# Routed attention and a mixture layer in one kernel: spare score banks in h's PSUM region, split cluster products, centroids on another queue, a new hand-written order

## The chip, the cores and the metric

The kernel runs on one core of one Trainium2 chip. The metric is device time in microseconds of one execution; smaller is better. The engines are TensorE (PE; its weight loads are shown as PEld), VectorE (DVE), ScalarE (ACT), GpSimd (POOL) and SyncE (SP), which here only issues transfers. SBUF holds 128 partitions; PSUM, where TensorE writes, has eight banks of 512 float32 per partition.

## The reference

Attention with 4 batches, 8 heads, 768 tokens and head size 64. Every query and key is assigned to the nearest of 16 centroids of its head, and a query sees only the keys of its own cluster. The result, 3072 tokens of 512, goes through a layer with a softmax-weighted activation and a layer norm.

```
q_n, k_n, c_n = each divided by its own norm
q_assign = argmax(q_n . c_n);  k_assign = argmax(k_n . c_n)
scores = q k^T / 8, where q_assign == k_assign, else -1e9
x = softmax(scores) v            # (3072, 512)
h = x w_in                       # (3072, 1024)
solu = h * softmax(h)
ln = (solu - mean) / sqrt(var + 1e-6) * g_ln
out = ln w_out                   # (3072, 512)
```

## The kernel before

**Tiling.** Heads are worked in pairs: 4 batches of 4 pairs, written b.p. A pair's queries and keys lie in one of six `qk` buffers with rows for the 64 features and, beneath them, one-hot rows of the cluster. The product of two such columns holds the score and a large constant where the clusters agree, and the exponential with a bias of the same size then makes all other keys vanish. So the mask costs no instruction of its own, but scores of a pair can start only when its one-hot rows are placed.

**Scores.** They are made in 294 banks of up to 512 columns, in the fixed order of the list `BANKS` (line 254 on): 24 banks for pair 0.0, then 54 for the pairs 0.1 to 0.3 (first 18 banks for the token thirds 0 and 1 of all three, six of a pair and third at a time, so that pair 0.1 has banks 24 to 35, pair 0.2 36 to 47, pair 0.3 48 to 59; then third 2 of each), then the other batches. TensorE writes a bank (S, line 582), ScalarE takes its exponential (E, line 588), and TensorE multiplies it with v (V, line 605); DVE divides by the sums (N, lines 617 and 630). The score banks come from a pool of three (`ps_s`, line 213), so bank i waits until the exponential of bank i - 3 has read its buffer (`ring_s`, line 1001).

**The layer.** It is done in 24 blocks f of 128 tokens. x is turned by a DMA transpose (tx; the last one by TensorE, ptx); h is four pieces of two matmuls (h, line 691) into `hreg`, a PSUM region of three banks, of which even f use banks 0 and 1 and odd f banks 1 and 2. DVE takes the negative maximum (hm, line 697), ScalarE the exponential (ex, line 703), DVE the product u (line 710) and its statistics (bn, ag), GpSimd the scale (at, al), a DMA transposes u (tu; the last two blocks by TensorE, ptu), TensorE makes y in four parts of two matmuls (y, line 757), ScalarE or DVE scales it (sc), and SP sends it out (ou).

**Preparation of a pair.** Loads (ld, lv on SP); a transpose, by TensorE into `hreg` with a copy out for batch 0 (tp, line 384; xa, line 394), by DVE for the others (xt, line 408); four casts into `qk` (ca, lines 432 to 436); a product with the centroids (cl, lines 446 and 451) in PSUM; its turn, maximum, comparison and turn on DVE (tb, mx, oh, ot, lines 460 to 484); four copies that place the one-hot rows (pl, lines 496 to 503: TensorE's batch 0, line 496; else 503, or line 501 by DMA); a blank (bl, line 512); v's casts (cv, line 521). Pair 0.0 is done in two halves of its tokens. For pairs 0.1 to 0.3 the cluster product has 8 matmuls in a row, in float32, at one go.

**Weights.** w_in is loaded (li) and cast on GpSimd (wi, line 540). w_out is loaded (lo), DVE sums its rows weighted by g_ln (su, line 560), TensorE makes the mean of the sum with one matmul of 512 columns into bank 2 of `hreg` (me, line 565), and DVE subtracts it from each of eight blocks (ce0 to ce7, line 568).

**What sets the order.** The class `Weave` (line 23). Every operation is added once with its engine, what it needs and how it is emitted. `ORDER` gives, per engine, the sequence of kinds by hand: `S3 V2 h` means three score banks, two V, one h, each the next of its kind. `AWAY` moves single operations to another engine than their usual one. Each engine executes its queue strictly in that order; an instruction that waits holds everything behind it.

**Start.** SP issues the centroids' load (line 791), then loads of pair 0.0 (line 367) alternate between ScalarE's queue and SP's. DVE normalises the centroids (cn, lines 833 to 846, with one power on GpSimd, line 836); TensorE turns them (cp, line 855).

Of the kernel before, what the change touches and what calls it, by code (L numbers as in the profile page):

```python
# [22 lines left out]
class Weave:  # L23
# [6 lines left out]
        ld4 lv si ld3 lo lg ld3 lv ld lo ld3 lo lv ld4 lv lo li ld8 li3 tx ld4 tx ld2 lv3 tu ld7 tx  # L30
        tu ld8 tu ld3 ou ld lv3 tu ou ld ou ld9 tu ld9 ou tx tu ld tx ld5 lv ld7 tu lv tx ou tu ld7
        tu ou2 ld4 ou ld4 lv ld3 tu2 ld2 pl ou pl2 ld pl tx lv ld2 tu lv ou tx ou lv tu tx pl tu pl2
        ou pl tu2 ou tx tu ou tx3 ou tu2 tx ou tu ou2 tu2 ou6
    """
    ORDER["POOL"] = """
        ca3 cv2 pl bl ca2 pl2 ca2 pl2 ca2 pl z sg ca2 pl2 ca bl pl2 cv z cv ca pl ca2 cv4 pl2 bl pl
        ca3 z ca z2 wi4 ca2 pl4 ca cv3 pl2 at bl al pl2 bl ca cv at ca4 al ca at pl3 ca cv2 pl at al
        cv2 ca2 cv al cv at cv pl4 ca2 cv ca2 pl4 bl at al ca6 al pl3 ca at ca pl bl ca cv al pl ca
        cv pl3 at ca at bl ca5 al cv pl2 at bl pl2 cv al2 ca2 bl cv ca4 at2 al pl cv al pl2 ca pl ca
        pl bl po pl at ca pl ca cv2 pl bl ca2 at2 al2 at3 al2 at al at2 al2 at al2 at al2 at al  # L40
    """
    ORDER["PE"] = """
        wm tp2 cp tp cl tp fl4 cl fl tp2 S3 tp2 S cq S2 tp2 S3 cl V2 S V S2 tp2 gt S V3 S2 tp2 S3 cl
        S2 V2 S V S2 tp S2 tp S V S V S V S3 cl S2 V2 S2 V2 S3 V2 S2 V S V S2 cl S2 V2 S2 V2 S3 V2
        S2 V2 S3 V2 S2 V2 S2 me S2 V2 S2 V2 S2 cl S3 V4 S2 h S h S2 h2 S2 V2 S2 V2 S h2 V2 S2 h S V2
        S2 h2 S3 h V3 S2 y3 S y S2 V3 S2 h2 S3 V4 cl S h2 S2 y S V2 S2 y2 S2 y V S2 V h V S3 V h2 S
        V y V y S3 y V3 S2 V y S V S h S2 h2 S V S2 cl S3 V3 h y2 S V S2 y2 S2 V2 S cl V S3 V4 S h S
        V S2 h S h S2 cl S V2 S2 V2 y2 S2 V2 S V2 S2 y S y S2 V3 S V S2 h2 S h2 S2 h2 S V S V3 y2 S
        y S y h2 S3 V cl V h S2 cl S2 V3 h S3 V3 S h2 S2 y4 S2 V h V3 S3 V h V S2 h S h S V S h S y3
        S3 V4 h V S2 h S y S h S h V2 S cl V2 S3 cl V2 S3 y2 S2 y S V2 h S y V2 S3 V2 cl S2 h2 S3 V  # L50
        y4 S V3 S2 y S y S2 V3 S2 V S y2 S3 V3 S V S h2 S h S2 V h S V2 S h S2 V h S y3 V S3 V y h2
        S2 V2 S V S cl V2 S2 h V h S2 h S h V S2 h S y2 V3 S V2 S2 h S h S2 h V S2 V3 y h V S3 h y V
        S2 h2 V S2 h S V y2 h V2 S3 y2 S2 V h2 S2 V y2 S V2 S2 h y h S2 h2 S2 V3 y S2 V S h2 V3 S V
        h2 S3 y4 h2 S3 V h2 S V3 y2 h y2 V S3 h2 V h y4 h V2 h y4 h2 ptx y4 h2 y3 h2 y ptu2 y7 ptu2
        y5
    """
    ORDER["DVE"] = """
        cn cb tb mx oh ot pl3 tb mx oh ot xa2 cf ca2 bl tb mx oh gk ot N pl su xa su tb mx oh xa ot
        su xa N xt su pl tb mx N oh bl ot xt N su tb su pl N su2 N mx oh ot N xt2 ce2 N ce2 tb N ce3
        hm ce N u mx oh ot N hm xt bn2 ag u xt N bn hm bn xt ag tb u mx N bn oh ot xt2 hm bl N bn u  # L60
        ag xt bn2 ag sc hm N tb mx oh ot u bn2 N xt tb mx bl xt oh N hm ot tb N u mx ag N xt oh bn
        ot N bn xt hm xt ag u xt bn2 ag hm tb N u mx tb oh bn N ot hm xt bn u sc xt N ag mx hm oh
        bn2 u xt2 N hm ag ot tb xt tb N mx u mx xt oh bn ot bn tb N ag bn hm bn sc mx N cv xt oh2 N
# [12 lines left out]
        ca0.0.0.1.1 sc23.0 xa0.0.0.1 xa0.0.1.0 xa0.1.0.0 xa0.1.0.1 xa0.2.0.0 xa0.2.0.1 xa0.2.1.0  # L76
        xa0.2.1.1 xa0.3.0.0
    """.split(), "ACT"))
    AWAY.update(dict.fromkeys("""
        bl0.0.1 bl0.2 bl1.2 bl1.3 bl3.3 ca0.0.1.1.1 ca0.1.0.0 cv3.0.0 cv3.1.0 cv3.3.0 cv3.3.1  # L80
        pl0.0.0.1.1 pl0.1.1.0 pl0.2.0.1 pl0.3.0.0 sc10 sc17 sc19 sc2 sc6 sc9 tu22.0
    """.split(), "DVE"))
    AWAY.update(dict.fromkeys("""
        ca0.0.1.1.0 pl0.0.1.0.0 pl0.0.1.1.0 pl1.0.0.0 pl1.0.0.1 pl1.0.1.0 pl1.0.1.1 pl1.1.0.0
        pl1.1.0.1 pl1.1.1.0 pl1.1.1.1 pl1.2.0.0 pl1.2.0.1 pl1.2.1.0 pl1.2.1.1 pl1.3.0.0 pl1.3.0.1
        pl1.3.1.0 pl1.3.1.1 pl2.0.0.0 pl2.0.0.1 pl2.0.1.0 pl2.0.1.1 pl2.1.0.0 pl2.1.0.1 pl2.1.1.0
        pl2.1.1.1 pl2.2.0.0 pl2.2.0.1 pl2.2.1.0 pl2.2.1.1 pl2.3.0.0 pl2.3.0.1 pl2.3.1.0 pl2.3.1.1
# [1153 lines left out]
```

## Time and profile before

| | us |
|---|---|
| timed runs: median (lowest to highest) | 228.2 (227.93 to 229.53) |
| the profiled execution, its own time | 229.23 |
| its span in the profile | 227.2 |
| PE busy | 216.9 |
| DVE busy | 201.0 |
| ACT busy | 195.0 |
| POOL busy | 132.3 |
| exponentials of the scores (L588), 294 | 152.0 |
| matmuls of the scores (L582), 636 | 93.5 |

The span runs from the first to the last instruction; some 2 us lie outside it. Matmul records overlap one another, so a sum of their durations is more than what they take of the engine. In the view by stretch each engine has its busy time in that stretch, with the count of instructions. In the view of waits a line says which instruction waited for which, the total in us, how often, and the longest. In the chain a line is a start, a length and what the chain passed through. In a list of instructions the columns are start, length, engine, line, operation, output<-input, count, and in brackets the idle time before it with what ended it. In the groups they are busy time and mean ns, then the idle time ahead.

### The profile page before, as it was taken

To read this page: it belongs to the slowest core of one execution; us is meant where nothing else is said; L and a number is where in the kernel's file an instruction comes from. 1 tells how busy PE (TensorE), PEld (TensorE's weight loads), DVE (VectorE), ACT (ScalarE), POOL (GpSimd) and SP (SyncE) were. 2 spreads that over 40 slices of the span, in tenths; PEclk is the share of its full clock that TensorE was granted. 3 is DMA by queue.
4 is the path that set the end of the run, shared out by engine and by line. 5 is a ranking of instruction groups with operands and counts; after the bars stand their busy time and mean duration, and the time that the engine had idled before them with its cause. 6 is when DMAs were issued, how large, how long until landed. Compare 5 with 4: busy or idle time off the path is not lost.

```text
span 227.2 us, 6588 instructions
## 1 busy us (share of the span) xinstructions
PE 216.9 (95%) x2394; PEld 147.8 (65%) x2424; DVE 201.0 (88%) x353; ACT 195.0 (86%) x378; POOL 132.3 (58%) x256
## 2 busy tenths in 40 slices
PE   6999988999999999999999999999999999999993
PEld 2566655666777767686567766687677677675452
DVE  2699999999999899898999989899899969798991
ACT  3599989999999999999888999899999999974352
POOL 4587799982498589386949742663818403213311
PEclk9999999999999999999999999999999999999999
DMA  6999989188898999999999979778944441396722
GB/s 157 315 365 230 280 185 302 40 156 248 143 169 144 240 205 193 132 194 151 174 193 208 209 135 185 158 145 192 211 90 110 94 116 28 80 130 178 182 91 106
DMA packets 125232, 39.00 MB, mean 172 GB/s; under 512 B 115081, under 2 KB 119953, under 8 KB 125201
## 3 DMA queue, kind: packets, MB, share of 16 engines
q1 hardware_dynamic: 123456, 38.06, 80.3%
q10 hardware_dynamic: 1744, 0.52, 0.9%
q8 instruction: 19, 0.31, 0.7%
q14 instruction: 13, 0.10, 0.1%
HBM read 23.11 MB, written 6.29 MB: 129 GB/s over the span
## 4 chain that ended last, share of the span: by engine, by line
PE 72%; DVE 13%; DMA 7%; SPq 3%; issue 2%; ACT 1%; DVEq 0%
PE sps L582 20%; PE hreg L691 16%; PE yps L757 14%; PE ops L605 12%; PE csc L451 4%; DMA raw<-in_k_dram 3%; DMA raw<-in_q_dram 2%; PE hreg L384 2%; DVE w_out_c L568 2%; DMA xT<-x 2%; SPq L400 2%; DVE xt L408 2%; DVE oh L478 2%; DVE w_sum L560 1%; DVE x L630 1%
## 5 line engine op out<-in xcount | busy, mean ns | idle before, releaser
L588 ACT ACTIVATE e<-sps 128x512 bf16<-128x512 f32 (+1 forms) x294 | 152.0, 595 | 12.0 <-PE sps L582 10.1
L582 PE MATMUL sps<-qk 96*128 96x256 bf16 (+5 forms) x636 | 93.5, 264 | 1.6 <-DVE qk L496 0.6
L582 PEld LDWEIGHTS <-qk 96*128 96x128 bf16 (+1 forms) x636 | 59.6, 121 | 26.4 <-issue 7.6
L605 PEld LDWEIGHTS <-e 128*128 128x128 bf16 x1152 | 49.6, 97 | 12.5 <-issue 3.5
L605 PE MATMUL ops<-v,e 128*128 128x65 bf16 x1152 | 54.2, 193 | 0.8 <-DVE x L630 0.6
L691 PE MATMUL hreg<-w_in_sb,xT 128*128 128x512 bf16 x174 | 49.0, 378 | 1.7 <-DMA xT<-x 0.4
L757 PE MATMUL yps<-w_out_c,uT 128*128 128x512 bf16 x172 | 45.8, 379 | 0.8
L503 POOL COPY qk<-oht 32x384 f32<-32x384 f32 (+1 forms) x45 | 21.9, 487 | 19.8 <-DVE oht L484 16.4
L710 DVE TENSOR_TENSOR u<-e_sb,hreg 128x1024 bf16<-128x1024 bf16 (+1 forms) x25 | 29.1, 1168 | 2.8 <-ACT e_sb L703 2.6
L697 DVE TENSOR_REDUCE nmax<-hreg 128x1 f32<-128x1024 f32 x24 | 29.2, 1217 | 2.5 <-PE hreg L691 2.0
L721 DVE BATCH_NORM_STATS2 bs<-u 128x6 f32<-128x512 bf16 x48 | 31.2, 675 | 0.2
L434 POOL CAST qk<-xt 64x768 bf16<-64x768 f32 (+1 forms) x32 | 26.7, 834 | 5.3 <-ACT xt L394 3.9
L703 ACT ACTIVATE e_sb<-hreg,nmax 128x1024 bf16<-128x1024 f32 x24 | 26.9, 1120 | 3.0 <-DVE nmax L697 2.9
L757 PEld LDWEIGHTS <-uT 128*128 128x128 bf16 x200 | 18.1, 97 | 14.8 <-DMA uT<-u 0.8
L436 POOL TENSOR_SCALAR qk<-xt 64x768 bf16<-64x768 f32 (+1 forms) x31 | 26.3, 849 | 2.1
L691 PEld LDWEIGHTS <-xT 128*128 128x128 bf16 x192 | 17.0, 97 | 10.4 <-DVE w_out_c L568 0.6
L408 DVE STREAM_TRANSPOSE xt<-raw 128x768 f32<-128x768 f32 x24 | 22.7, 957 | 0.0
L737 POOL TENSOR_SCALAR esq<-es,mv 128x1 f32<-128x1 f32 x24 | 8.2, 340 | 24.3 <-DVE mv L725 24.1
L731 POOL TENSOR_SCALAR es<-esum 128x1 f32<-128x1 f32 x24 | 6.0, 251 | 26.9 <-ACT e_sb L703 26.3
L630 DVE TENSOR_TENSOR x<-ops,den 128x256 bf16<-128x256 f32 (+1 forms) x39 | 19.0, 486 | 1.3
L521 POOL CAST v<-vf 128x384 bf16<-128x384 f32 x28 | 14.0, 514 | 6.1 <-DMA vf<-in_v_dram 4.9
L775 ACT ACTIVATE y<-yps,alpha 128x512 f32<-128x512 f32 x17 | 11.7, 690 | 6.6 <-PE yps L757 5.8
(77 smaller groups left out, 178.9 us busy)
## 6 DMA issues: line engine op xcount, KB each, us to landing
vf<-in_v_dram SPq DMA_DIRECT2D x16, 384.0 KB, 4.7
out_dram<-y SPq DMA_DIRECT2D x23, 256.0 KB, 2.4
raw<-in_q_dram SPq DMA_DIRECT2D x50, 96.0 KB, 3.2
raw<-in_k_dram SPq DMA_DIRECT2D x50, 96.0 KB, 2.8
w_g<-in_moe_w_out_dram SPq DMA_DIRECT2D x4, 512.0 KB, 6.7
w_st<-in_moe_w_in_dram SPq DMA_DIRECT2D x4, 512.0 KB, 4.9
raw<-in_q_dram SPq DMA_DIRECT2D x3, 384.0 KB, 6.8
raw<-in_k_dram SPq DMA_DIRECT2D x3, 384.0 KB, 7.2
```

The costliest lines, as they stand in the source:

```text
L408: nc.vector.transpose(xt[:], raws[b, p, i][:].rearrange("p j c -> p (j c)"))
L434: VEC[e].tensor_copy(dst, src)
L436: VEC[e].tensor_scalar(dst, src, scalar1=inv_C, scalar2=1.0, op0=Alu.mult, op1=Alu.mult)
L582: nc.tensor.matmul(sps_[n, k][:, c0:c0 + w], side(b, h // 2, 1, h % 2, keys)[r], side(b, h // 2, 0, h % 2, slice(s0 * P, s0 * P + w))[r])
L588: nc.scalar.activation(es[n, k][:, :w], sps_[n, k][:, :w], Act.Exp, scale=exp_scale, bias=-exp_scale)
L605: nc.tensor.matmul(opss[g][:, s, :VW], es[n, k][:, c0:c0 + P], v1[slot(b, h // 2)][:, h % 2, kt, :VW], start=(kt == 0), stop=(kt == n_t - 1))
L691: uses(nc.tensor.matmul(hreg[:, at(f, f2)[1], :], xTs[f][:, dc, :], w_in_sb[:, dc, f2 * FF2:(f2 + 1) * FF2], start=(dc == 0), stop=(dc == ...
L697: uses(nc.vector.tensor_reduce(ff[f, "nmax"][:], pair_of(f), axis=AXY, op=Alu.max, negate=True), *both(f))
L703: uses(nc.scalar.activation(ff[f, "e"][:], pair_of(f), Act.Exp, bias=ff[f, "nmax"][:], accum_out=ff[f, "esum"][:]), *both(f))
L710: uses(nc.vector.tensor_tensor(ff[f, "u"][:, r], ff[f, "e"][:, r], pair_of(f)[:, r], op=Alu.mult), *both(f)[r])
L721: nc.vector.bn_stats(ff[f, "bs"][:, f2, :], ff[f, "u"][:, f2, :])
L757: ins = nc.tensor.matmul(dst, ff[f, "uT"][:, at(f, f2)[0] * (n_fc // 2) + c, :], w_out_c[:, fc, cols], start=(fc == fcs[0] and part % 2 == ...
```

## The change

1. **Spare banks.** Of banks 24 to 65 in `BANKS`, two of every five are written into banks 0 and 1 of `hreg` instead of the pool of three. These banks of `hreg` are otherwise used by the turned tokens of batch 0 (until then) and by h (afterwards). A bank in the pool waits for the exponential of the bank three before it in the pool; a bank in `hreg` for the one five before. The first h waits for the last exponential that reads its bank.
2. **Cluster products** of pairs 0.1 to 0.3 become two operations, ck and cl, of four matmuls each, and other work can stand between them.
3. **The mean of w_out** becomes two matmuls of 256 columns, me0 and me1.
4. **The centroids** are loaded from GpSimd's queue, ahead of its iota, and no longer by SP.
5. **`ORDER` and `AWAY`** are written anew.

```
-    nc.sync.dma_start(out=c_all[:], in_=centroids.rearrange("h c d -> (h c) d"))
+    nc.gpsimd.dma_start(out=c_all[:], in_=centroids.rearrange("h c d -> (h c) d"))
...
-    def clusters(b, p, hf):
+    def clusters(b, p, hf, hh=None):
...
-            for hh, c in ((hh, c) for hh in range(2) for c in range(4)):
+            for c in range(4):
...
-    def mean_w_out():
-        uses(nc.tensor.matmul(hreg[:, 2, :], g_mean[:], w_sum[:]), 2)
+    def mean_w_out(x):
+        cols = slice(x * FF2 // 2, (x + 1) * FF2 // 2)
+        uses(nc.tensor.matmul(hreg[:, 2, cols], g_mean[:], w_sum[:, cols]), 2)
...
+    spare_from, spare_to = 24, 66
+    slots = {BANKS[i]: (i - spare_from) % 5 for i in range(spare_from, spare_to)
+             if (i - spare_from) % 5 < 2}
...
+        j = slots.get((n, k))
+        sps_[n, k] = (ps_s.tile([P, 512], F32, name="sps", tag="sps") if j is None else
+                      hreg[:, j, :])
...
-        if i >= ring_s:
-            nd.append("E{}.{}".format(*BANKS[i - ring_s]))
+        aft = ["S{}.{}".format(*BANKS[i - 1])] if i else []
+        if (n, k) in slots:
+            j = slots[n, k]
+            nd += [of_bank[j]] if j in of_bank else [
+                x for m, x in enumerate(ring_h[-3:], len(ring_h) - 3) if m % 3 == j]
+            aft += [] if j in of_bank else last_tp[-1:]
+            of_bank[j] = f"E{n}.{k}"
+        else:
+            nd += of_ring[-ring_s:][:1] if len(of_ring) >= ring_s else []
+            of_ring.append(f"E{n}.{k}")
```

What the new `ORDER` and `AWAY` do to the queues, as far as it is spoken of below (numbers are b.p, or the block f):

```
VectorE loses     pl0.1.1.0 pl0.2.0.1 pl0.3.0.0 (line 496, to GpSimd)   bl0.0.1 bl0.2 bl1.2 bl1.3 bl3.3 (to GpSimd)
                  ca0.0.1.1.1 (half cast, to ScalarE)   ca0.1.0.0 (to GpSimd)   sc6 sc17 sc19 and tu22.0 (to ScalarE)
VectorE gains     three of pair 0.0's small pl, net   ca0.1.1.1 ca3.2.1.0   bl2.3   sc1 sc12 sc13 sc18 sc23.1
                  cv0.0.1 cv0.2.1 ahead of the first hm;  behind it cv1.2.0 cv1.3.0 cv2.2.0 cv3.0.1 cv3.1.1 cv3.2.0,
                  without cv3.1.0 and cv3.3.1
VectorE, order    before: ... ot1.0 N6 xt xt ce0 ce1 N7 ce2 ce3 tb N8 ce4 ce5 ce6 hm0 ce7
                  after:  ... ot1.0 xt xt N6 ce0 ce1 ce2 ce3 N7 ce4 ce5 tb ce6 ce7 N8 hm0
                  (N6 is what the first tx waits for)
ScalarE           two more half casts of pair 0.0, between its first copies; E and xa as before in number
GpSimd, order     before: ... bl0.3 pl0.3.0.1 ca1.0.0.0 ca1.0.0.1 ca1.0.1.0 z3 ca1.0.1.1 z4 z5 wi0 wi1 wi2 wi3
                  after:  ... bl0.3 cv0.3.1 pl1.0.1.1 wi0 wi1 z4 wi2 wi3 ca1.0.0.1   (pl1.0.* needs ot1.0)
                  casts ca0.2.1.0, ca0.2.1.1 and ca0.3.0.0 stand behind bl0.1 instead of ahead of it
SP                pl1.0.1.0, one pl of pair 2.3 and some of pairs 3.2 and 3.3 by DMA; those of pair 3.0 no longer
TensorE, tail     before: ptx23 y19(4) h23.0 y20.0-2 h23.1 y20.3 ptu22 y21(4) y22.0-2 ptu23 y22.3 y23(4)
                  after:  ptx23 y18.0 h22.1 y18.1-3 h23.0 y19(4) h23.1 ptu22.0 y20.0-1 ptu22.1 y20.2-3 y21(4)
                          ptu23.0 y22(4) ptu23.1 y23(4)
```

More of the change, by code (lines that the diff above doesn't have):

```diff
@@ L47 @@
[L47 to L51, printed above, removed]
@@ L581, in scores @@
             keys = slice(kt * P, (kt + 1) * P) if by_token(b) else slice(kt, S, n_t)
[L582 to L583 removed]
+            ins = nc.tensor.matmul(sps_[n, k][:, c0:c0 + w], side(b, h // 2, 1, h % 2, keys)[r],
+                                   side(b, h // 2, 0, h % 2, slice(s0 * P, s0 * P + w))[r])
+            if j is not None:
+                uses(ins, j)
     def expo(n, k):
@@ L1198 @@
             [f"lo{fc // 2}"] + ([f"su{fc - 1}"] if fc else ["gk"]))
-    add("me", "PE", 0.9, 36, lambda e: mean_w_out(), [f"su{n_fc - 1}", "sg"] + [
+    for x in range(2):
+        add(f"me{x}", "PE", 0.45, 36 + x, (lambda e, x=x: mean_w_out(x)),
+            ["me0"] * x + [f"su{n_fc - 1}", "sg"] + [
         x for j, x in enumerate(ring_h[-3:], len(ring_h) - 3) if j % 3 == 2], last_tp[-1:])
```

117 lines of the change are left out of this document (64 added, 53 removed).

## Prediction

> **What bounds the kernel now.** I read the page's head first, then busy time by stretch, the waits of ScalarE in the stretch that the change touches, the chain that ended last, and the grouped instructions with shapes kept apart.
>
> ```profile
> span 227.2 us, 6588 instructions
> PE 216.9 (95%) x2394; PEld 147.8 (65%) x2424; DVE 201.0 (88%) x353; ACT 195.0 (86%) x378; POOL 132.3 (58%) x256
> ```
>
> ```profile
> core 0: us, PE busy (x) PEld busy (x) DVE busy (x) ACT busy (x) POOL busy (x), PEclk, DMA share, GB/s
> 0.00:10.00 10.00, 8.13 (x39) 4.03 (x39) 3.87 (x18) 4.13 (x8) 4.51 (x22) 1.00 0.81 221
> 25.00:30.00 5.00, 4.89 (x71) 3.18 (x69) 4.92 (x10) 4.15 (x9) 4.05 (x7) 1.00 1.02 304
> 30.00:35.00 5.00, 3.88 (x53) 2.12 (x49) 4.73 (x11) 4.36 (x10) 4.67 (x9) 1.00 0.92 139
> 35.00:40.00 5.00, 4.37 (x73) 3.32 (x69) 4.88 (x8) 4.65 (x11) 4.65 (x7) 1.00 1.05 333
> 60.00:70.00 10.00, 9.89 (x110) 6.98 (x111) 9.90 (x18) 9.98 (x21) 7.72 (x14) 1.00 1.07 157
> 80.00:100.00 20.00, 19.84 (x241) 13.98 (x242) 18.73 (x35) 19.12 (x38) 14.67 (x28) 1.00 1.14 179
> 180.00:200.00 20.00, 19.79 (x246) 14.06 (x249) 16.09 (x27) 18.57 (x37) 3.52 (x10) 1.00 0.42 93
> ```
>
> ```profile
> ACT e L588 <- PE sps L582: 2.6, 8, 0.9
> ```
>
> ```profile
> 49.78 1.97 DVE w_out_c L568 x3
> 51.76 1.13 DVE nmax L697
> 219.34 1.29 DVE u L710 x2
> ```
>
> The granted clock is 1.00 everywhere, so no term comes from it. Three regimes follow. Up to 10 us the loads set the pace. From there to the first max over h (chain: 51.76 us) VectorE is the tightest: 4.92 of 5, 4.73 of 5 and 4.88 of 5, while TensorE drops to 3.88 and ScalarE to 4.15; the chain runs through VectorE's w_out_c and nmax. ScalarE lost only 2.6 us there to late scores. From 60 us on TensorE is 98 to 99% busy (9.89 of 10, 19.84 and 19.79 of 20). So a microsecond won before the first h is kept only while TensorE stays that full later, and the tail again hangs on VectorE (u, at 219.34).
>
> **The change, part by part.** The profiled execution took 229.23 us, its span 227.2, so 2.0 lie outside the span. The sum is made on the span; the median of the three timed runs, 228.2, is 1.0 below the profiled one, and I apply the same difference to it.
>
> *1. Centroids on GpSimd's queue.*
>
> ```profile
> 0.72 0.40 SPq L791 DMA_DIRECT2D c_all<-in_centroids_dram  x1
> 1.19 0.41 SPq L367 DMA_DIRECT2D raw<-in_q_dram  x1
> 2.78 0.23 DVE L833 CUSTOM_DVE_ANT_0 c_n<-c_all 128x64 f32<-128x64 f32 x1 [1.46 <-DMA c_all<-in_centroids_dram]
> 4.55 0.29 DVE L846 TENSOR_SCALAR c_n<-c_all,c_inv 128x128 f32<-128x128 f32 x1
> 5.82 0.23 PEld L855 LDWEIGHTS cps<-ident_f,c_n 128*128 128x128 f32 x1
> 11.06 0.65 PE L582 MATMUL sps<-qk 80*128 80x384 bf16 x3
> ```
>
> ```profile
> 1.65 3.58 DMA raw<-in_k_dram
> ```
>
> The chain starts with SP's load of k at 1.65 us, which stands behind the centroids in SP's queue; SP's q load follows the centroids at 1.19, 0.47 after 0.72. Without them all of SP's loads issue 0.47 earlier. How much earlier they land is between 0 (the DMA engines are 0.81 busy in these 10 us, and the bytes stay) and 0.47; I take 0.3, nearer the issue, since the chain names the load from its issue on. The price is the centroids' arrival. c_n is ready at 4.84 and TensorE takes it at 5.82, so cover is 0.98, or 0.68 once the k load lands 0.3 earlier. Issued by GpSimd, the load delays iota and the memsets ahead of c_s. The trace has no such issue; SP's takes 0.40, and landing took 2.06. A price of up to 0.68 is hidden; twice SP's issue would still be. Range of this part: 0.47 won to 0.4 lost; taken: 0.3 won.
>
> [...]
>
> *2. VectorE's path to the first h.*
>
> ```profile
> L496 DVE COPY qk<-oht 32x384 f32<-32x384 f32 x3 | 2.2, 746 | 0.1
> L503 DVE COPY qk<-oht 32x192 f32<-32x192 f32 x3 | 1.1, 360 | 0.1
> L521 DVE CAST v<-vf 128x384 bf16<-128x384 f32 x4 | 1.5, 398 | 0.0
> L436 DVE TENSOR_SCALAR qk<-xt 64x384 bf16<-64x384 f32 x1 | 0.8, 801 | 0.0
> L512 DVE MEMSET qk<- 16x384 f32 x4 | 1.5, 378 | 0.5
> L512 DVE MEMSET qk<- 16x192 f32 x1 | 0.2, 218 | 0.1
> L777 DVE TENSOR_SCALAR y<-yps,alpha 128x512 f32<-128x512 f32 x6 | 4.5, 744 | 1.3 <-issue 0.8 <-PE yps L757 0.6
> L434 DVE CAST qk<-xt 64x768 bf16<-64x768 f32 x1 | 1.1, 1075 | 0.0
> L568 DVE SCALAR_TENSOR_TENSOR w_out_c<-w_g,g_ln,hreg 128x512 bf16<-128x512 f32 x8 | 5.6, 736 | 0.0
> ```
>
> Ahead of the first max VectorE loses three one-hot copies of pairs 1 to 3 (2.2 us), one half cast (0.8) and two memsets (0.22 + 0.38), in all 3.6. It gains three small one-hot copies (1.1), two casts of v (0.8) and ce7, which now stands in front of the max (0.74), in all 2.64. A whole-pair cast only changes its operand. Net 0.96 less; with part 1's 0.3 the first max ends 1.3 earlier than 52.89, near 51.6. The one-hots of pairs 1 and 2 move back in VectorE's order, behind the four small copies and a cast of v. I cost that at nothing, because GpSimd, which now copies them all, has three casts of pairs 2 and 3 behind pair 1's copies that stood ahead of them. If that cover is gone, pair 2's scores come late by what VectorE's order lost, and ScalarE with them: up to the 1.8 of those five.
>
> *3. Two more banks, split cluster products, split mean.* They add no TensorE column: 16 records per pair in one piece become twice 8, and the mean's one matmul becomes two of half width. They take away waits.
>
> ```profile
> 28.73 3.53 ACT L588 ACTIVATE e<-sps 128x512 bf16<-128x512 f32 x7 [0.85 <-PE sps L582]
> 38.48 8.74 ACT L588 ACTIVATE e<-sps 128x512 bf16<-128x512 f32 x17 [0.17 <-PE sps L582]
> 26.77 1.54 PE L446 MATMUL csc<-xt,w_out_c 128*32 128x384 f32 x16
> 33.02 0.39 PE L582 MATMUL sps<-qk 96*128 96x256 bf16 x2 [0.56 <-DVE qk L512]
> ```
>
> An exponential costs 8.74 / 17 = 0.514 in a row. The largest wait, 0.85 at 28.73, follows the 1.54 us cluster product at 26.77: two more banks of lead and a split product would hide it. TensorE's own wait of 0.56 at 33.02 is for one-hot work (the blank, on VectorE), which no bank shortens; it goes with part 2. Alone this is worth 0 to 2.6, all waits for scores; but VectorE's 51.6 binds first, so beyond part 2 it adds nothing: 0. It is needed, though: ScalarE must save the same 1.3 to be there in time. The first h may write only after the last exponential that reads its banks (score banks 64 and 65); the h stands behind score bank 68, so at most one exponential, 0.5, could show.
>
> *4. After the first h.* VectorE gets 4 casts of v (1.6), one whole-pair cast (1.1) and, net, one and a half scalings of y (1.1), and loses two memsets (0.76) and one copy of uT (about 0.4): 2.6 more. Between 60 and 200 us it idles: 0.10 of 10, then 1.27 and 3.91 of 20 in the rows quoted. Bounds: 0 to 2.6 lost. I take 0.2, nearer the idle: TensorE, not VectorE, is the full one there.
>
> *5. The tail.* Three of y20's four parts move behind the last h. One part is two matmuls:
>
> ```profile
> 69.70 0.86 PE yps L757 x4
> 216.85 1.23 DVE L697 TENSOR_REDUCE nmax<-hreg 128x1 f32<-128x1024 f32 x1
> 211.68 1.23 DVE L697 TENSOR_REDUCE nmax<-hreg 128x1 f32<-128x1024 f32 x1
> ```
>
> In the chain four take 0.86 (first row), so a part is 0.43 and the three are 1.3. They fill the time in which TensorE waits for u23 (219.34). But the last maxima already stand 5.17 apart (211.68, 216.85), and max, exponential and u follow each other; only what waited for TensorE can come sooner. 0 to 1.1 won, taken 0.3.
>
> **Sum:** -0.3 - 0.96 - 0 + 0.2 - 0.3 = -1.4. Span 225.8, profiled execution 227.8, median 226.8.
>
> **Rivals.**
> A. *The front gains nothing.* GpSimd now waits for batch 1's one-hot (ot1.0) with all four casts of w_in behind that wait, and the first transposed x goes out only after two VectorE transposes more:
>
> ```profile
> 41.28 4.32 POOL L540 CAST w_in_sb<-w_st 128x1024 bf16<-128x1024 f32 x4
> 42.76 0.58 DVE L484 STREAM_TRANSPOSE oht<-oh 128x384 bf16<-128x384 bf16 x1
> 48.76 0.59 PE L691 MATMUL hreg<-w_in_sb,xT 128*128 128x512 bf16 x2
> ```
>
> If ot1.0 ended at 43.34 as now, the casts would end no sooner than 43.34 + 4.32 = 47.7, a microsecond ahead of where h starts now (48.76). It is for ot1.0 to come about 1.3 sooner; what it comes less, h loses. For it: a new order with a wait ahead of four long casts. Against: VectorE's removed copies lie ahead of ot1.0. Then: 228.2.
> B. *VectorE binds the middle* (the other side). Part 4's 2.6 all land on the path between 60 and 180 us: -1.4 - 0.2 + 2.6 = +1.0, or 229.2; if also part 2 is lost, 230.2. It decides from 1.6 of the 2.6 on. For it: 9.90 of 10 at 60 us. Against: idle time in every later row.
> C. *All waits go.* ScalarE's 2.6 vanish in full and VectorE follows, the head gives 0.47, the tail 1.1: -4.2 at most; about -3.2 if a quarter is lost, 225.0. Against: VectorE's sum has only 0.96.
>
> **How the numbers follow.** Forecast 0.47 (its own range: 225.7 with the winning ends of parts 1 and 5 and nothing lost in 4, to 227.9 with part 1's loss and no tail), A 0.22, B 0.16, C 0.15. A measurement of this kernel tells about 1%, 2.3 us, from no change: faster is below 225.9, slower above 230.5. Faster: C and a strip of the forecast, together 0.22. Slower: B with part 2 lost and more, most of B, 0.14. Within: 0.64. Range 225.0 (C) to 229.6 (past B), leaving some 0.2 out.
>
> **What would show it.** Head: SP's k load issued near 1.2, the first scores near 10.7 instead of 11.06, c_n ready before TensorE wants it. Part 2: first max near 50.4 instead of 51.67. Part 3: the 0.85 wait at 28.73 gone, short waits for one-hots left. Part 4: TensorE still at 98% and more from 60 to 200. Tail: the last h followed by seven more y parts of f 20 and 21 and no idle TensorE before u23. I am wrong if the first max stands where it stood, or if it is early and TensorE has new idle time after 60 us.

## The result and the profile after

The changed kernel took 230.47 us, the median of 20 runs (229.09 to 231.97), against 228.22 for the kernel before (20 runs). That is 2.25 us slower, where 1.4 faster was forecast, and above the top of the range. The ratio, 1.0086 with a 95% interval of 1.0062 to 1.011, is taken over the fast runs and puts the loss at 2.0 us. The profiled execution took 230.38 us, about its median. The one of before lay 1.0 above its median, so the two traces show 1.1 of the 2.2.

The page's head and busy time by stretch, after:

```profile
span 228.3 us, 6643 instructions
PE 217.9 (95%) x2426; PEld 148.7 (65%) x2426; DVE 200.4 (88%) x356; ACT 195.4 (86%) x379; POOL 131.8 (58%) x254
```

```profile
core 0: us, PE busy (x) PEld busy (x) DVE busy (x) ACT busy (x) POOL busy (x), PEclk, DMA share, GB/s
0.00:10.00 10.00, 6.69 (x31) 3.41 (x31) 3.38 (x16) 4.26 (x9) 4.45 (x21) 0.88 0.88 251
30.00:40.00 10.00, 8.30 (x108) 5.64 (x106) 9.13 (x15) 7.65 (x16) 9.07 (x15) 0.83 0.89 251
60.00:200.00 140.00, 139.55 (x1636) 99.75 (x1635) 129.33 (x221) 131.22 (x251) 83.80 (x157) 1.00 0.83 160
```

The engines' sums are those of before. The first ten microseconds changed most: TensorE has 6.69 busy where it had 8.13. From 60 us on it is full (139.55 of 140). The timeline of the head shows why (columns: start, duration, engine, line; in brackets the idle time before and what ended it; lines are those of the changed kernel, whose L844 and L866 are L833 and L855 of before):

```profile
1.23 0.77 POOL L802 DMA_DIRECT2D c_all<-in_centroids_dram  x1 [0.80 <-POOLq L1253]
2.10 0.26 POOL L809 IOTA idx_i<- 128x128 int32 x1
4.71 0.23 DVE L844 CUSTOM_DVE_ANT_0 c_n<-c_all 128x64 f32<-128x64 f32 x1 [2.09 <-DMA c_all<-in_centroids_dram]
5.03 0.57 POOL L847 TENSOR_TENSOR c_s<-c_nsq,halves 128x1 f32<-128x1 f32 x1 [0.95 <-DVE c_nsq L844]
6.61 0.29 DVE L857 TENSOR_SCALAR c_n<-c_all,c_inv 128x128 f32<-128x128 f32 x1
6.95 0.33 PE L866 MATMUL cps<-ident_f,c_n 128*128 128x128 f32 x1 [1.96 <-DVE c_n L857]
11.81 0.65 PE L589 MATMUL sps<-qk 80*128 80x384 bf16 x3
```

GpSimd issues the centroids' load at 1.23 (SP did at 0.72), takes 0.77 for it (SP 0.40), and VectorE can begin c_n at 4.71, 1.93 later than the 2.78 of before. c_n is ready at 6.90 instead of 4.84; TensorE stands 1.96 us for it, and the first scores come at 11.81 instead of 11.06. A second new wait shows in the list of waits (total, times, longest):

```profile
PE cps L866 <- DVE c_n L857: 2.0, 1, 2.0
PE sps L589 <- POOL qk L496: 1.7, 1, 1.7
```

The second is TensorE's wait before pair 2's scores, for one-hot copies that GpSimd now makes. VectorE's first max over h begins at 53.1, where it was 51.67:

```profile
L708 DVE TENSOR_REDUCE nmax<-hreg x1: 1225/1225/1225, 53.1 to 53.1; 128x1 f32<-128x1024 f32 x1
```

### The profile page after: what moved, and what is told of

Its sections match the earlier page's. It is cut to its first block, busy times and chain, and to the rows that moved or that the text cites. A ratio compares the mean times of both kernels' runs of the same rounds, so it can differ in the third digit from the quotient of the medians.

```text
span 228.3 us, 6643 instructions
## 1 busy us (share of the span) xinstructions
PE 217.9 (95%) x2426; PEld 148.7 (65%) x2426; DVE 200.4 (88%) x356; ACT 195.4 (86%) x379; POOL 131.8 (58%) x254
## 4 chain that ended last, share of the span: by engine, by line
PE 76%; DVE 12%; POOL 5%; ACT 3%; issue 2%; DVEq 0%; POOLq 0%; ACTq 0%
PE sps L589 21%; PE hreg L702 16%; PE yps L768 15%; PE ops L616 13%; PE csc L452 5%; ACT e L597 2%; PE idle_p L816 2%; PE hreg L589 2%; PE hreg L383 1%; POOL qk L433 1%; DVE oht L484 1%; DVE nmax L708 1%; POOL qk L496 1%; DVE xt L393 1%; DVE y L788 1%
## 5 line engine op out<-in xcount | busy, mean ns | idle before, releaser
L597 ACT ACTIVATE e<-sps 128x512 bf16<-128x512 f32 (+1 forms) x276 | 144.2, 606 | 11.6 <-PE sps L589 9.4
L589 PE MATMUL sps<-qk 96*128 96x256 bf16 (+5 forms) x600 | 89.1, 265 | 2.0 <-POOL qk L496 1.7
L589 PEld LDWEIGHTS <-qk 96*128 96x128 bf16 (+1 forms) x636 | 61.1, 121 | 29.4 <-issue 6.7
L616 PE MATMUL ops<-v,e 128*128 128x65 bf16 x1152 | 53.6, 194 | 0.6 <-DVE x L641 0.6
L702 PE MATMUL hreg<-w_in_sb,xT 128*128 128x512 bf16 x192 | 53.3, 379 | 0.0
L768 PE MATMUL yps<-w_out_c,uT 128*128 128x512 bf16 x184 | 48.6, 379 | 0.1
L435 POOL TENSOR_SCALAR qk<-xt 64x768 bf16<-64x768 f32 (+1 forms) x29 | 24.3, 836 | 2.0
L751 POOL TENSOR_TENSOR alpha<-esq,halves 128x1 f32<-128x1 f32 x24 | 13.5, 562 | 2.0
L786 ACT ACTIVATE y<-yps,alpha 128x512 f32<-128x512 f32 x16 | 11.1, 693 | 3.9 <-PE yps L768 2.3
L742 POOL TENSOR_SCALAR es<-esum 128x1 f32<-128x1 f32 x24 | 5.1, 220 | 15.1 <-ACT e_sb L714 14.5
```

The lines of the kernel that those rows point to most:

```text
L435: VEC[e].tensor_scalar(dst, src, scalar1=inv_C, scalar2=1.0, op0=Alu.mult, op1=Alu.mult)
L589: ins = nc.tensor.matmul(sps_[n, k][:, c0:c0 + w], side(b, h // 2, 1, h % 2, keys)[r], side(b, h // 2, 0, h % 2, slice(s0 * P, s0 * P + w) ...
L597: ins = nc.scalar.activation(es[n, k][:, :w], sps_[n, k][:, :w], Act.Exp, scale=exp_scale, bias=-exp_scale)
L616: nc.tensor.matmul(opss[g][:, s, :VW], es[n, k][:, c0:c0 + P], v1[slot(b, h // 2)][:, h % 2, kt, :VW], start=(kt == 0), stop=(kt == n_t - 1))
L702: uses(nc.tensor.matmul(hreg[:, at(f, f2)[1], :], xTs[f][:, dc, :], w_in_sb[:, dc, f2 * FF2:(f2 + 1) * FF2], start=(dc == 0), stop=(dc == ...
L768: ins = nc.tensor.matmul(dst, ff[f, "uT"][:, at(f, f2)[0] * (n_fc // 2) + c, :], w_out_c[:, fc, cols], start=(fc == fcs[0] and part % 2 == ...
```

## The experiments

Each kernel ran beside the kernel before on the same chip. The medians of before run from 228.22 to 229.56, on one chip alone from 228.35 to 229.56, so ratios are compared, not times.

| kernel | ratio to before | 95% interval |
|---|---|---|
| changed kernel | 1.0086 | 1.0062 to 1.011 |
| changed kernel, once more | 1.0098 | 1.0064 to 1.0131 |
| changed, centroids first on SP | 0.9998 | 0.9974 to 1.0022 |
| the same, second chip | 1.0012 | 0.9982 to 1.0042 |
| changed, centroids on SP behind the raw loads | 1.0173 | 1.0139 to 1.0208 |
| changed, centroids on ScalarE's queue | 1.0051 | 1.0018 to 1.0085 |
| before, centroids on GpSimd | 1.0065 | 1.0042 to 1.0089 |
| the same, second reading | 1.0045 | 1.0016 to 1.0073 |
| changed, SP, idle load on GpSimd | 1.0058 | 1.003 to 1.0087 |
| the same, second chip | 1.0032 | 1.0002 to 1.0062 |
| before, idle load on GpSimd | 1.0067 | 1.003 to 1.0104 |
| the same, second chip | 1.0108 | 1.0065 to 1.015 |
| before, idle memory sets on GpSimd | 1.0175 | 1.0117 to 1.0234 |
| changed, idle matmuls over the wait | 1.0109 | 1.0079 to 1.0139 |
| changed, pair 2's copies sooner on GpSimd | 1.0153 | 1.0116 to 1.0189 |
| changed, SP, two copies by VectorE | 1.0041 | 1.0016 to 1.0066 |
| changed, SP, no spare banks | 1.0057 | 1.0029 to 1.0084 |
| changed, SP, one cast by ScalarE | 0.9964 | 0.9935 to 0.9993 |
| the same, second reading | 0.9946 | 0.9914 to 0.9978 |

**Is it the centroids?** The theory: the centroids land too late, and TensorE's wait for c_n is the loss. The rivals: the halved clock that follows the wait, the new order's wait at 32 us, and GpSimd's issuing as such. First only the queue was undone in the changed kernel, and only the queue was changed in the kernel before.

```diff
-    nc.gpsimd.dma_start(out=c_all[:], in_=centroids.rearrange("h c d -> (h c) d"))
+    nc.sync.dma_start(out=c_all[:], in_=centroids.rearrange("h c d -> (h c) d"))
```

> The changed kernel with one part undone: the centroids are loaded by SP again, first in its queue; everything else, the new order too, as in the changed kernel. Theory of two late arrivals (the changed kernel loses to a late landing of the centroids, 4.71 against 2.78 us, and to pair 2's one-hot rows at 31 to 34 us, and TensorE's clock is halved for some 3.5 us after each of the two gaps): c_n ready near 4.9, TensorE's wait of 1.96 us ahead of the centroids' turn gone, granted clock 1.0 in the first 15 us, first scores near 11.0 instead of 11.7, time 0.8 to 1.6 below the changed kernel's 230.5, so 229.3. Rival, the new order loses after the first h and TensorE, full from there on, takes back whatever the start gains: within 0.4 of 230.5.

> The kernel before with one part of the change alone: the centroids are loaded from GpSimd's queue. Theory of two late arrivals: the centroids land near 4.7 instead of 2.8, TensorE stands still for about 1 to 2 us ahead of their turn, its clock is halved for some 3 us behind that, first scores near 11.7 to 12, time 0.8 to 1.6 above before, so 229.4. Rival (the loss is the new order's): within 0.4 of 228.2, because the later stretches have slack that takes the start up.

Measured: 0.9998 and 1.0065. The queue alone accounts for all of the change's loss, more than the 0.8 to 1.6 us expected of it, and for 1.5 us of loss in the old order too; everything else in the change nets nothing that the interval (0.9974 to 1.0022) could tell from none. The head with SP (timeline):

```profile
0.72 0.40 SPq L802 DMA_DIRECT2D c_all<-in_centroids_dram  x1
2.88 0.23 DVE L844 CUSTOM_DVE_ANT_0 c_n<-c_all 128x64 f32<-128x64 f32 x1 [1.56 <-DMA c_all<-in_centroids_dram]
3.20 0.57 POOL L847 TENSOR_TENSOR c_s<-c_nsq,halves 128x1 f32<-128x1 f32 x1 [0.43 <-DVE c_nsq L844]
4.64 0.29 DVE L857 TENSOR_SCALAR c_n<-c_all,c_inv 128x128 f32<-128x128 f32 x1
5.46 0.27 PE L866 MATMUL cps<-ident_f,c_n 128*128 128x128 f32 x1
7.11 0.55 PE L383 MATMUL hreg<-ident_f,raw 128*128 128x128 f32 x3 [0.17 <-DMA raw<-in_k_dram]
9.82 0.65 PE L589 MATMUL sps<-qk 80*128 80x384 bf16 x3
```

c_n is ready at 4.93 and TensorE takes it at 5.46 without waiting. The first scores come at 9.82, where the trace of before has 11.06, but not all of that is the queue's. Three turning matmuls take 0.55 us here, and 0.90 in the trace of before:

```profile
7.82 0.90 PE L384 MATMUL hreg<-ident_f,raw 128*128 128x128 f32 x3
```

That is what they take in the changed kernel where its granted clock is 0.50 (0.90 at 8.55 us), although the clock's column has 1.00 for these 10 us of before. So the column doesn't show how TensorE starts, and the prediction's "granted clock is 1.00 everywhere" doesn't hold for the head. Starts of the first scores can be compared only between traces whose turns take the same. On a later chip the kernel with SP ran beside the changed kernel:

> The changed kernel with the centroids on SP's queue once more, now beside the changed kernel itself and the idle load, so that the three stand on one chip. Theory one, the loss is the later landing that c_n waits for: the ratio to the kernel before is 1.000 as before (0.998 to 1.002). Theory two, the new order itself costs about 1 us, and the first reading of 0.9998 was one chip's: 1.004 to 1.006.

> The changed kernel unaltered, beside the kernel with the centroids on SP's queue. Theory one: 1.008 to 1.010 of the kernel before, and 1.5 to 2 us over the kernel with SP. Theory two: 1.007 to 1.010 as well, but less than 1 us over the kernel with SP.

1.0012 and 1.0098: theory one, with 0.0086 of 229 us, or 2.0 us, between the two. In both of these traces the last three of the first turns take 0.90, and the first scores start at 10.92 and 12.54, 1.6 apart.

**Landing or issuing?** SP issues the centroids here, but behind its four raw loads, so that they land late and GpSimd issues nothing:

```diff
-    nc.gpsimd.dma_start(out=c_all[:], in_=centroids.rearrange("h c d -> (h c) d"))
     for hf in range(2):
...
                 load_tokens(0, 0, i, hh, 3 * hf, 3 * hf + 3, (nc.scalar, nc.sync)[hh])
+    nc.sync.dma_start(out=c_all[:], in_=centroids.rearrange("h c d -> (h c) d"))
     load_v(0, 0)
```

> The changed kernel with the centroids on SP's queue behind its four first raw loads: issued near 2.7 us and landed near 4.7, as late as GpSimd's load landed (4.71), with the raw loads as early as in the changed kernel, and nothing issued by GpSimd. Theory one, the landing that c_n waits for is the cost: TensorE stands some 2 us before the centroids' turn (cps) and the ratio to the kernel before is 1.007 to 1.010, as the changed kernel has. Theory two, GpSimd's issue is the cost: 1.000 to 1.003, as with the centroids first on SP.

```profile
3.63 0.34 SPq L806 DMA_DIRECT2D c_all<-in_centroids_dram  x1
6.89 0.23 DVE L844 CUSTOM_DVE_ANT_0 c_n<-c_all 128x64 f32<-128x64 f32 x1 [5.57 <-DMA c_all<-in_centroids_dram]
9.13 0.47 PE L866 MATMUL cps<-ident_f,c_n 128*128 128x128 f32 x1 [3.67 <-DVE c_n L857]
```

The landing came later than meant (c_n begins at 6.89, not 4.7), and the loss grew with it: 1.0173, beyond both ranges. TensorE takes c_n at 5.46 and 5.49 in the two traces with SP first, at 6.95 and 7.09 in the two of the changed kernel, and at 9.13 here. So against SP first some 1.5 and 3.7 us of lateness go with losses of 2.0 and 3.8 us (0.0168 of 229). About one microsecond is lost for each, with no GpSimd load at all. That late landing is a sufficient cause is shown. How exact the proportion is stays open: the granted clock was lowered in all six runs here (0.978 to 0.993), and a part of the 3.8 can be the clock's.

Does GpSimd's issuing cost anything more? A load of 48 of the 64 columns into a tile that nothing reads, with the centroids themselves on SP:

```diff
     nc.sync.dma_start(out=c_all[:], in_=centroids.rearrange("h c d -> (h c) d"))
+    c_too = const.tile([P, 48], F32, name="c_too")
+    nc.gpsimd.dma_start(out=c_too[:], in_=centroids.rearrange("h c d -> (h c) d")[:, :48])
```

> The changed kernel with the centroids on SP's queue, and a second load by GpSimd's queue at the place where the change put its own: 48 of the 64 columns of the centroids into a tile that nothing reads. Theory one, the whole loss is the later landing, which c_n waits for: the time is 228.4, as with SP alone (228.0 to 228.8). Theory two, what costs is that GpSimd issues the load (0.77 us ahead of the iota, and the descriptors), so that the identity, the first turns and the casts on GpSimd come later: 229.4 to 230.5, near the 230.3 of the changed kernel.

> The changed kernel with SP's centroids and an idle load of 48 columns by GpSimd, once more. Theory one, only the landing counts: within 0.3 us of the kernel with SP alone. Theory two, GpSimd's issue counts, by the memory sets and casts that it holds up or by its own descriptors beside the raw loads: 1 to 1.5 us over the kernel with SP alone, near the changed kernel.

1.0058 and 1.0032. The first lies in theory two's range; the second, read on the chip of the second reading with SP (1.0012), is only 0.5 us above that, nearer to theory one. In the second's trace (timeline) c_s, a step of c_n's chain that GpSimd makes, moves from 3.20 to 4.04, behind the iota that the load pushed back, although the centroids had landed by 2.83:

```profile
1.24 0.77 POOL L804 DMA_DIRECT2D c_too<-in_centroids_dram  x1 [0.81 <-POOLq L1255]
2.11 0.26 POOL L811 IOTA idx_i<- 128x128 int32 x1
2.83 0.24 DVE L846 CUSTOM_DVE_ANT_0 c_n<-c_all 128x64 f32<-128x64 f32 x1 [0.19 <-DMA c_all<-in_centroids_dram]
4.04 0.58 POOL L849 TENSOR_TENSOR c_s<-c_nsq,halves 128x1 f32<-128x1 f32 x1
5.49 0.48 DVE L859 TENSOR_SCALAR c_n<-c_all,c_inv 128x128 f32<-128x128 f32 x1
```

So the load's place in GpSimd's queue makes c_n about 1 us late by itself (5.97 for 4.93), and TensorE takes it at 6.03, some 0.5 later than with SP alone. In the changed kernel that is no second sum: the landing is later still, and GpSimd stands idle for 0.95 us before c_s there. Whether GpSimd's issuing costs anything besides the lateness of c_n is not settled by losses of 0.5 and 1.2 us. The same idle load in the kernel before, and the real load there once more beside it:

> The kernel before with its centroids on SP's queue, and the same idle load of 48 columns by GpSimd. Theory one, only the landing counts: the time of the kernel before, ratio 0.999 to 1.001, where with the centroids themselves on GpSimd it was 1.0065. Theory two, the issue on GpSimd counts: 1.004 to 1.007.

> The kernel before with SP's centroids and the idle load of 48 columns by GpSimd, once more, now beside the real one. Theory one, the landing: at most 1.002. Theory two, GpSimd's issue: 1.005 to 1.008, as the real one, and as the first reading of 1.0067 had it.

> The kernel before with only the centroids on GpSimd's queue, once more. Both theories: 1.005 to 1.008, as read before (1.0065).

1.0067 and 1.0108 for the idle load, 1.0045 for the real one (1.0065 before, and 1.005 to 1.008 expected): an idle load costs the old order at least as much, against theory one. Then GpSimd work without a transfer:

```diff
+    c_too = const.tile([P, 48], F32, name="c_too")
+    for _ in range(8):
+        nc.gpsimd.memset(c_too[:], 0.0)
```

> The kernel before, with eight idle memory sets on GpSimd (0.1 us each) ahead of the iota in place of the idle load. Theory one, the idle load cost by the place it takes in GpSimd's queue, since c_s and with it c_n come later: with the iota some 0.8 us later the ratio is 1.002 to 1.006. Theory two, it cost by its transfer beside the raw loads: 0.999 to 1.001.

1.0175, more than either theory had; the sets took 1.50 us, not 0.8, and the iota came at 2.25. But the head lost little: first scores at 11.12 for 11.06. TensorE's timeline has the rest far behind, at a transposed x, first here and then in the kernel before:

```profile
11.12 0.65 PE L582 MATMUL sps<-qk 80*128 80x384 bf16 x3 [0.27 <-DVE qk L503]
...
105.09 1.89 PE L691 MATMUL hreg<-w_in_sb,xT 128*128 128x512 bf16 x4 [2.52 <-DMA xT<-x]
```

```profile
102.56 0.81 PE L691 MATMUL hreg<-w_in_sb,xT 128*128 128x512 bf16 x3 [0.37 <-DMA xT<-x]
```

SP issued that transpose at 104.4 instead of 101.6, the eight raw loads ahead of it, from 92 us on, having taken 7.1 us to go out (4.33 and 2.73) instead of 6.0 (3.76 and 2.24), and a single one after them 1.67 instead of 0.57. So in this trace the loads around 100 us have no slack. The two traces of the idle load don't have that wait; TensorE waits 0.7 and 1.5 us for a transposed u in them. Why SP's issues took longer is not settled; nor is the price of work at GpSimd's head in the order before, nor, therefore, how much of the real load's 1.0 to 1.5 us there is the landing's. The finding for the changed kernel rests on its own order, with SP first and SP behind the raw loads.

**The clock.** In the changed kernel's profiled run the granted clock is halved right after the two waits (columns as in the table by stretch):

```profile
7.00:8.00 1.00, 0.85 (x8) 0.60 (x12) 0.29 (x1) 0.36 (x1) 0.00 (x0) 0.78 0.98 378
8.00:9.00 1.00, 1.00 (x10) 0.45 (x3) 0.32 (x1) 0.95 (x3) 0.82 (x2) 0.50 1.03 396
35.00:36.00 1.00, 1.00 (x17) 0.93 (x16) 0.98 (x1) 1.00 (x3) 0.99 (x2) 0.50 0.96 313
```

Was that the loss? Eighteen idle matmuls fill the first wait:

```diff
-        wm tp2 cp tp cl tp fl4 cl fl tp2 S3 cq
+        wm tp2 fl18 cp tp cl tp fl4 cl fl tp2 S3 cq
```

> The changed kernel with 18 idle matmuls of 256 columns on TensorE between the first turned tokens and the centroids' turn: the wait for the late centroids stays, but TensorE is not idle in it. It takes the clock apart from the wait. If the halved clock behind the gap is a part of the loss: granted clock 1.0 from 7 to 11 us, cluster product and second half's turn as fast as in the kernel before, first scores near 11.3 instead of 11.7 and 0.4 to 0.9 off the time, so 229.9. If only the wait matters: first scores at 11.7 and 230.5 within 0.3.

The clock stayed up (0.999 in the profiled run) and the first scores came at 11.18, even before the 11.3 of the first theory, but the ratio was 1.0109, no better than 1.0086. The idle matmuls also ran on until TensorE took c_n at 7.34, 0.4 later than in the changed kernel, so this run alone doesn't separate the two cleanly. The clock on record for every run does it better. Where only runs at 0.996 or more are compared, the changed kernel is at 1.011 (three runs beside those of before on one chip), the kernel with SP at 1.0006 and 1.0004. In the changed kernel's first 20 runs the eight at 0.996 or more average 230.56 us, the twelve below 230.57. So the loss is there without the fallen clock.

That doesn't make a fallen clock free. In each of the five groups of runs of the kernel before, those below 0.996 took on average 0.9 to 1.2 us longer than the others. In the changed order a clock that falls behind the second wait shows its price too: 0.65 us, in the table under part 2.

In the changed kernel's trace the halved clock stands behind waits of 1.96 and 1.70 us. Not every wait of that length has it: behind the 1.69 us of the first trace with SP the clock is 1.00 from 30 to 40 us, in the second trace with SP it is 0.83. The clock of the changed kernel's 20 runs lies between 0.985 and 1.0. What decides in which runs it falls is not shown.

**The wait at 32 us.** GpSimd's order was changed so that pair 2's one-hot copies come before two more casts:

```diff
-        ca3 pl2 sg bl cv bl ca4 z2 ca pl4 z bl cv2 ca5 pl4 bl ca2 cv2
+        ca3 pl2 sg bl cv bl ca4 z2 ca pl4 z bl cv2 ca3 pl4 bl ca4 cv2
```

> The changed kernel with GpSimd's queue turned round in one place: the four one-hot copies of pair 0.2 and their blank stand in front of the casts ca0.3.0.1 and ca0.3.1.0 instead of behind them. The late centroids stay. Theory of two late arrivals: pair 2's copies end near 31.5 instead of 33.7, TensorE's gap of 1.7 us at 32 to 33.7 shrinks below 0.5, the clock stays at 1.0 from 34 to 39 us (0.50 in the changed kernel), time 1.0 to 2.0 below 230.5, so 229.0. Rival (TensorE has spare time there, the loss is later): within 0.4 of 230.5. Second rival, the casts moved back make pair 3 late by as much: the gap moves to about 37 to 38 us and the time stays.

1.0153: pair 2's wait went, and a larger one stands before pair 3's scores:

```profile
41.43 0.38 PE L589 MATMUL sps<-qk 80*128 80x256 bf16 x2 [2.31 <-POOL qk L496]
```

GpSimd is nearly full in that stretch (9.07 of 10 from 30 to 40 us in the changed kernel), and the new order only moved its lateness, as the second rival had it. Next, two of the four copies went to VectorE, where they stood before the change:

```diff
-        ca3 pl2 sg bl cv bl ca4 z2 ca pl4 z bl cv2 ca5 pl4 bl ca2 cv2
+        ca3 pl2 sg bl cv bl ca4 z2 ca pl4 z bl cv2 ca4 pl2 bl ca3 cv2
...
-        ot N su2
+        ot pl2 N su2
```

> The changed kernel with the centroids on SP's queue, where TensorE still stands 1.69 us at 30.0 us of the span and 0.7 us more until 36 us, both times behind one-hot copies by GpSimd (L496). Here VectorE makes two of pair 0.2's four copies right after its transposed one-hots (L484), and GpSimd makes the other two one cast sooner. Theory one, TensorE's waits of the first 60 us are what is left to gain: the 1.69 us shrink to at most 0.5 and the time falls from 228.4 to about 227.3 (226.9 to 227.8). Theory two, VectorE sets the first h: its two copies (1.1 us) push the w_out sums and centrings back by as much, the first max moves from 50.4 to 51.5 in the profile and the time stays at 228.4 (228.0 to 228.8).

1.0041, worse than SP's centroids alone and above what either theory allowed; the first max came at 51.8, near theory two's 51.5. TensorE's waits became these:

```profile
29.73 0.35 PE L616 MATMUL ops<-v,e 128*128 128x65 bf16 x6 [1.23 <-POOL qk L496]
33.94 0.36 PE L616 MATMUL ops<-v,e 128*128 128x65 bf16 x6 [1.09 <-DVE x L641]
```

VectorE is full there as well (9.76 of 10 from 30 to 40 us): its copies held up the normalising that TensorE's next V products wait for. ScalarE, which stands idle 1.5 us in that gap, was the engine with room. It took one of the casts:

```diff
-        ca0.0.0.0.0 ca0.0.0.0.1 sc23.0
+        ca0.3.0.0 ca0.0.0.0.0 ca0.0.0.0.1 sc23.0
...
-        cv2 ca5 pl4
+        cv2 ca4 pl4
...
-        xa E3 xa2 E6 xa2 E3 xa2 E63
+        xa E3 xa2 E6 xa2 E3 xa2 E3 ca E60
```

> The changed kernel with the centroids on SP's queue, and one of the five casts ahead of pair 0.2's one-hot copies on GpSimd's queue (0.83 to 1.0 us) made by ScalarE, behind the first three exponentials of the third bank set. Theory one, TensorE's wait of 1.69 us at 30 us of the span is worth its time: it shrinks to about 0.7, and the ratio to the kernel before falls from 1.000 to 0.996 (0.994 to 0.998). Theory two, ScalarE's cast holds up exponentials by as much, or the wait moves on to pair 0.3's copies: 0.999 to 1.003.

> The changed kernel with SP's centroids and one of pair 0.3's casts on ScalarE, once more. Theory one, TensorE's wait at 30 us was worth its time: 0.994 to 0.998 again. Theory two, the first reading was one chip's: 0.999 to 1.003, as with SP's centroids alone.

0.9964 and 0.9946: this version beats both kernels, by 0.8 and 1.2 us against the one before. Against SP alone it is 1.15 us (0.0050). The clock has a share in that: with the shorter wait none of 24 runs fell below 0.997, where ten of the 24 with SP alone had 0.985 to 0.993. Among runs at 0.996 or more the ratios are 0.9973 and 0.9957, so that 0.9 of the 1.15 us remains. TensorE's wait with SP alone, and then with ScalarE's cast:

```profile
31.71 0.81 PE L589 MATMUL sps<-qk 80*128 80x256 bf16 x6 [1.69 <-POOL qk L496]
```

```profile
31.21 0.81 PE L589 MATMUL sps<-qk 80*128 80x256 bf16 x6 [0.84 <-POOL qk L496]
```

**The spare banks.** With SP's centroids, all scores go through the ring of three:

```diff
-             if (i - spare_from) % 5 < 2}
+             if (i - spare_from) % 5 < 0}
```

> The changed kernel with the centroids on SP's queue and no bank of h's region given to scores: all of them go through the ring of three, in the new order. Theory one, the banks give nothing, since TensorE is 98.9% busy from 60 to 200 us before the change too: 228.4 as with them (228.0 to 228.8). Theory two, the banks do help and another part of the new order takes it back: without them scores wait for exponentials between 30 and 80 us and the time rises by 1 us or more, to 229.4 or above.

1.0057 where 0.9998 and 1.0012 were read with them: theory two. The banks are worth about 1.2 us (0.0052 of 229, read on different chips) in the new order, which was laid out for them; the banks alone in the old order were not tried.

**ScalarE's queue for the centroids.**

```diff
-    nc.gpsimd.dma_start(out=c_all[:], in_=centroids.rearrange("h c d -> (h c) d"))
+    nc.scalar.dma_start(out=c_all[:], in_=centroids.rearrange("h c d -> (h c) d"))
```

> The changed kernel with the centroids issued by ScalarE's queue, ahead of its own first raw loads. Theory one, only the landing counts: the centroids land some 2.0 us after their issue at 0.72, c_n starts by 3.0, and the time is that with SP, 228.4, or up to 0.4 less as SP's first raw load goes out 0.46 us earlier (227.9 to 228.6). Theory two, what counts is which raw load the first turns wait for: ScalarE's four raw loads go out 0.4 to 0.5 us later, a turn waits for one of them, and the time is 228.8 to 229.3.

1.0051, slightly above theory two's range, but not by its mechanism as far as the trace shows. ScalarE's own raw loads and its table load do come later (1.18 and 3.28 us, where the changed kernel has 0.72 and 2.90), and so does TensorE's first turn, at 4.25 for 3.87 with SP:

```profile
3.28 1.28 ACT L822 ACT_TABLE_LOAD   x1 [3.28 <-DMA c_all<-in_centroids_dram]
...
4.25 1.40 PE L383 MATMUL hreg<-ident_f,raw 128*128 128x128 f32 x6 [0.34 <-DVE c_norm L853]
```

Yet TensorE takes c_n at 5.49, as with SP, and the first scores come at 10.25, between the two traces with SP (9.82 and 10.92). What stands out is the clock: ten of the twelve runs have 0.975 to 0.992, and the two at 0.998 took 228.63 and 228.79 us, no more than the median of before, 228.99. Why the clock fell so often with this queue is open.

## Why the prediction was wrong, step by step

*Part 1 (0.3 won forecast) is the step that failed.* It said that cover was 0.98, or 0.68 once the k load came earlier, and that "a price of up to 0.68 is hidden; twice SP's issue would still be". The price was 2.06: c_n ready at 6.90 for 4.84. I bounded it by SP's issue of 0.40, but the landing is what changed, and the rows that I had bounded it by were SP's alone. Measured: 0.51 from the later start of the issue, 0.13 in the steps from c_s to c_n, and 1.4 between issue and landing, which took 3.5 instead of 2.06 (the list of DMA issues, KB and us to landing):

```profile
c_all<-in_centroids_dram POOLq DMA_DIRECT2D x1, 32.0 KB, 3.5
```

What the 1.4 us more from issue to landing consist of is open.

The cover was wrong too. The 5.82 at which TensorE took c_n was set by the k load, which TensorE waited 0.70 for. In the changed kernel the turns were done by 4.99, so cover was 0.15 (4.99 - 4.84), and 2.06 - 0.15 makes the 1.9 that TensorE stood. The earlier k load, the winning side of the step, shows in this trace, and there it only lengthened the wait; in the second trace of the changed kernel TensorE waits 0.76 for k, as before, and 0.87 for c_n. Part 1 measured 2.0 lost (1.0086 against 0.9998), 2.3 away from the forecast.

*Part 2 (0.96 won) gave nothing, since the cost that it put at nothing took it.* With SP's centroids the first max begins at 50.4 in the first trace, the very time that the prediction named for it:

```profile
L708 DVE TENSOR_REDUCE nmax<-hreg x2: 1212/1218/1225, 50.4 to 55.9; 128x1 f32<-128x1024 f32 x2
```

That agreement is luck. It comes from the head of this one trace, as the stretch from the first scores to the first max shows (us; the clock is that of 30 to 40 us):

| trace | first scores | first max | between | clock |
|---|---|---|---|---|
| before | 11.06 | 51.67 | 40.61 | 1.00 |
| changed kernel | 11.81 | 53.07 | 41.26 | 0.83 |
| the same, once more | 12.54 | 53.78 | 41.24 | 0.83 |
| SP first | 9.82 | 50.42 | 40.60 | 1.00 |
| the same, second chip | 10.92 | 52.17 | 41.25 | 0.83 |
| SP, one cast by ScalarE | 10.16 | 49.92 | 39.76 | 1.00 |
| the same, second reading | 10.36 | 50.13 | 39.77 | 1.00 |
| SP, no spare banks | 10.39 | 52.56 | 42.17 | 1.00 |

With SP the stretch is as long as before where the clock stays up, and 0.65 longer where it falls behind TensorE's wait. None of the 0.96 shows. The copies moved to GpSimd were costed at nothing, with the bound "If that cover is gone, pair 2's scores come late" by up to 1.8. It was gone: in the first trace with SP pair 2's transposed one-hots are ready at 26.78, but GpSimd, behind its casts, copies them from 29.14 to 31.66. TensorE waits 1.69 for them, and the same wait stands in the changed kernel (1.70). Taking 0.85 of it away, with ScalarE's cast, makes the stretch 0.84 shorter.

*Part 3 (0)* was too low in one sense: the banks are worth about 1.2 us to the new order, and without them the stretch in the table is 1.6 longer. ScalarE's wait of 0.85 at 28.73 went, and the wait for one-hots came in its place, so that the sum with part 2 is none.

*Part 4 (0.2 lost)* is not contradicted. With SP TensorE is busy for 137.95 and 137.62 of the 140 us from 60 on (138.01 before), and from the first max to the end of the span it is 176.2 and 175.5 (175.5 before). New idle time after 60 us, which the prediction had named as a sign of being wrong, is there once in each, 0.85 and 0.44 for a transposed u. Rival B, VectorE as the bound of the middle, did not come about. Rival A did not either: GpSimd does stand idle for pair 1.0's transposed one-hots ahead of the casts of w_in, 2.22 and 3.30 us, but the first h, at 47.11 and 48.82 (48.76 before), shows no wait for these casts.

*Part 5 (0.3 won)* gave nothing. The last four maxima over h start at 200.8 to 216.8 before and 200.1 to 215.0 with SP's centroids. The last y products, before and then with SP:

```profile
222.41 1.48 PE L757 MATMUL hreg<-w_out_c,uT 128*128 128x256 bf16 x12 [0.19 <-DVE uT L685]
```

```profile
220.91 2.17 PE L768 MATMUL hreg<-w_out_c,uT 128*128 128x256 bf16 x16
```

From the first of these maxima to the end it is 23.1 before (223.89 - 200.8) and 23.0 with SP (223.08 - 200.1). TensorE's idle 0.19 went, as forecast; the y parts behind the last h are only moved.

So parts 2 to 5 were forecast at 1.1 won and net 0.0 (0.9998 and 1.0012), part 1 at 0.3 won and cost 2.0: 1.1 + 2.3 make 3.4 of the 3.7 between 226.8 and 230.47. The rest is the difference between the loss by the ratio (2.0) and by the medians (2.25).

## What to carry to other kernels

When a load moves to a queue that the trace has never seen load anything, bound it by the whole way from issue to landing, and look at what set the time at which its data are taken: if that is moved up in the same change, the cover goes with it. Measure a term between two marks of one trace, here the first scores and the first max: heads of one kernel differed by 1.1 us between two traces. Where two engines are full in a stretch (here GpSimd with 9.07 and VectorE with 9.13 of 10 us), handing work from one to the other, or putting it in another order, moved the wait (it came back as one of 2.31 us, and as two of 1.23 and 1.09); look for the engine that is idle in the very gap. A change of several parts can hold a loss and a gain that hide one another: undo one part at a time.

## What the runs showed of the hardware

- A 32 KB load issued by GpSimd at the start took 0.77 us of its time and landed 3.5 to 3.7 us after its issue (six traces); by SP, first in its queue, 0.40 and 1.8 to 2.1. Put behind four raw loads in SP's queue, it took 3.2.
- The granted clock fell to 0.50 for some 3 us after TensorE waits of 1.7 to 2.0 us, in some runs and not in others: behind the wait of 1.7 at 30 to 34 us in the changed kernel and the second trace with SP, not in the first. There it cost 0.65 us up to the first max. Holding the clock up over the first wait with idle matmuls gained nothing that can be measured.
- In the first 10 us the clock's column can say 1.00 while matmuls take what they take at 0.50: three turns 0.90 us in the trace of before, 0.55 in one with SP.
- A memory set of 128x48 on GpSimd took 0.19 us (1.50 for eight).
- About 1.5 us of idle work at GpSimd's start cost the kernel before 1.7%, of which TensorE's trace shows 2.5 us as one wait for a transposing load at 105 us.
